# A fused attention, Fourier and MLP kernel: the last main row group is normalised behind its second product, under a new order of issue

## The chip, the cores and the metric

The kernel runs on one core of a Trainium2 chip. The metric is the device time of one launch in microseconds (us). The engines are TensorE (PE; its weight loads are shown as PEld), VectorE (DVE), ScalarE (ACT), GpSimd (POOL) and SyncE (SP), which only issues DMAs here.

## The reference, cut to what matters

```python
# q, k, v: (4, 4, 1088, 32); S1, S2: (8, 32); w_ch1: (128, 512); w_ch2: (512, 128)
phi  = lambda x: outer(S1 x, S2 x) per row, flattened to 64 features
kv   = einsum('bhsf,bhfd', phi(k), v);  z = sum over s of phi(k)
x    = (phi(q) kv) / (phi(q) z + 1e-6)        # laid out as (4, 1088, 128)
u    = x + real(fft(fft(x, axis=1), axis=2))
un   = (u - mean(u)) / sqrt(var(u) + 1e-6)    # over the 128 columns
out  = u + relu(un @ w_ch1) @ w_ch2           # (4, 1088, 128), float32
```

The mean is taken out by centring the first weight matrix (`cen`), so the kernel needs only the factor 1/sqrt(var + 1e-6) of each row, called its scale here. The scale is positive, so it may stand before or behind the ReLU.

## The kernel before, in words

There are four batches. For each batch b the kernel projects k (`kpr`), forms the 64 products of features (`kp`, four pieces), sums them against v on TensorE (`kv`, copied by `kvz`), does the same for q in two halves (`qf`, `qa`, `qp`), and multiplies both (`pnd`; `den`, `rden`, `x` divide). The Fourier step folds x over the columns and over the batch's two row halves (`df` and `eo`), multiplies with sine and cosine tables made on the chip (`s`), and copies the sum out (`z`); `zr` is its mirror for the second row half (two instructions of 272 columns), `zl` gathers the columns of the last rows (two small strided copies). The tables come from `t_turn`, `l_turn`, `d_turn` on POOL, `t_ph`, `l_ph`, `d_ph`, `t_pm`, `l_pm`, `d_pm` on DVE, and sines on ACT.

The MLP then works on ten groups g of rows. Groups 4 and 9 are the small last ones (128 rows each: the tails of two batches); the eight others are the main ones, 512 rows each; group 8 is the last main one (`TWO = 8`). For each group: `mix` adds x and the transform into PSUM (the tile is called u), `bn` and `var` take the statistics on DVE, `sd` a square root on ACT, `rc` a reciprocal on DVE, `un` writes u times the scale, rounded to bf16. The rounded rows are transposed: by a DMA for groups 0 to 6 (`xt`, line 635), by TensorE for 7, 8 and 9 (`tr`, then the copy `ut`). `ph` multiplies with the first weights, `rl` is the ReLU (each in two parts of 1024 columns), `po` multiplies with the second weights and adds onto u in PSUM, `fin` copies the sum to SBUF and `out` stores it. Group 8's u lies in two PSUM banks, so that its `po`, `fin` and `out` run in two halves.

PSUM has eight banks, and the table `BANK` says which bank a use has; a use waits until the bank's former readers are done. Nothing is scheduled at run time: the list `ORDER` is a written order of all steps, each engine gets its own steps in that order and runs them strictly so. `ENGINE` moves a step from its default engine. `FILL` puts multiplications of zeros ahead of a step on TensorE. `BEHIND` makes a load wait for an earlier load, `AFTER` makes one step wait for another without sharing data.

Of each engine's order before, what the change and the prediction touch: on PE `kv0 qf1.1 pnd0 kv1 qf2.1 pnd1 w1c qf3.1 kpr2 s0 ... po2 ph3.0 ph3.1 s3`; on DVE `bn0 var0 kvz2 rc0 un0 qp3.0`, with `zr0` on ACT and `zl0` on POOL; on POOL `kp3.1 kp3.0 kp3.3 kp3.2 w2b zl0`; at the end `mix8` on PE, then `bn8 var8 rc8 un8` on DVE with `sd8` on ACT, `tr8 ut8 ph8.1 rl8.1 ph8.0 ... po8.0 fin8.0 po8.1 fin8.1`.

Of the kernel before, what the change touches and what calls it, by code (L numbers as in the profile page):

```python
# [56 lines left out]
def program(nc, T, x, bank):  # L57
# [596 lines left out]
    def po(u, g, lo, hi):  # L654
        for t in range(lo, hi):
            for c in range(4):
                nc.tensor.matmul(ps(u, ut_at(g, t), [[1, 128]]), view(own("ht", g), (128 if g % 5 == 4 else 512) * c + 128 * t, [[1, 128]]),  # L657
                                 T("w2b")[:, c, :], start=False, stop=True, skip_group_check=True)
# [191 lines left out]
ld_vt1 c_kvz c_sgn kpr0.1 kt_pr c_v10 ld_q2.1 ld_v1.3 kt_ab kt_p qT1.0 ld_v1.0 qT1.1 ld_v1.1 ld_v1.2 ld_q2.0 qp0.1  # L850
ld_q3.1 kpr0.0 kab0 kp0.3 kp0.1 ld_k2 qt_T d_trig qf0.0 qa0.0 qp0.0 kT1 ld_q3.0 kp0.2 qf1.0 qa1.0 vc0 qt_f ld_w1 kp0.0
qp1.0 l_turn c_qtp kpr1 t_ph3 qt_a kab1 t_cos1 ld_v2.0 kv0 l_ph kvz0 kp1.1 vc1 qf1.1 ld_v2.3 qT2.1 ld_v2.1 ld_k3 qa1.1
qt_p kp1.2 t_sin1 kp1.3 ld_v2.2 l_pm l_sin pnd0 c_eo0 qT2.0 qT3.1 kp1.0 ld_v3.0 den0 kv1 c_eo2 c_eo1 kvz1 qp1.1 d_alt
qf2.1 rden0 x0 df0.1 kT2 qa2.1 l_cos pnd1 ld_v3.2 qT3.0 df0.0 den1 qp2.1 w1c eo0.0 ld_w2 w1b qf3.1 eo0.1 kpr2 qa3.1
kab2 rden1 x1 t_neg ld_v3.1 ld_v3.3 s0 qp3.1 kp2.0 qf2.0 kT3 vc2 kpr3 kp2.1 z0 kp2.3 mix0 kp2.2 qa2.0 df1.1 qp2.0
a_sqrt kv2 kab3 df1.0 eo1.0 bn0 eo1.1 zr0 kp3.1 kp3.0 qf3.0 var0 sd0 kvz2 rc0 un0 qa3.0 qp3.0 mix1 vc3 bn1 kp3.3 s1
var1 pnd2 sd1 z1 kp3.2 xt0 ph0.1 rl0.1 zr1 rc1 kv3 w2b zl0 den2 rden2 x2 df2.1 kvz3 df2.0 eo2.1 un1 ph0.0 mix2 xt1 zl1
rl0.0 bn2 var2 pnd3 eo2.0 sd2 rc2 s2 den3 rden3 x3 un2 z2 mix3 ph1.0 bn3 xt2 var3 po0 fin0 out0 rl1.0 sd3 ph1.1 ph2.0
rc3 un3 rl1.1 rl2.0 df3.0 zr2 df3.1 eo3.1 mix5 bn5 var5 zl2 ph2.1 rl2.1 po1 mix4 eo3.0 mix6 bn4 var4 sd5 po2 sd4 rc5
fin1 fin2 xt3 ph3.0 rl3.0 rc4 un4 un5 xt4 ph3.1 bn6 var6 sd6 rc6 xt5 un6 s3 z3 xt6 rl3.1 ph4.0 po3 zr3 rl4.0 ph5.0  # L860
rl5.0 po4 fin3 zl3 ph5.1 fin4 mix9 bn9 mix7 ph6.0 var9 rl5.1 sd9 bn7 out2 out3 out1 out4 rl6.0 var7 rc9 po5 un9 ph6.1
sd7 fin5 rc7 mix8 rl6.1 tr9 un7 ut9 ph9.0 tr7 rl9.0 po6 bn8 var8 ut7 sd8 rc8 fin6 ph7.0 rl7.0 un8 po9 out5 ph7.1 rl7.1
out6 fin9 tr8 ut8 ph8.1 rl8.1 ph8.0 out9 po7 fin7 out7 rl8.0 po8.0 fin8.0 po8.1 fin8.1 out8.1 out8.0
# [38 lines left out]
```

## Time and profile before

| What | us |
|---|---|
| median of the 3 runs (82.08, 82.40, 84.12) | 82.4 |
| the profiled execution, its own time | 82.32 |
| its span, from the first to the last instruction | 80.4 |
| busy: PE, PEld, DVE, ACT, POOL | 69.6, 52.0, 65.0, 49.5, 45.2 |

Of the 3 runs two lie within 0.4% of each other and one is 2.1% above the median. The profiled execution has 1.9 us around its span. PE is the busiest engine; a busy PE means that a matmul was in its pipeline, not that the array was full.

### The profile page before, as it was taken

What the parts mean: (1) busy time and instruction counts of PE and PEld (TensorE: products, weight loads), DVE (VectorE), ACT (ScalarE), POOL (GpSimd) and SP (SyncE); (2) the same over time, 40 slices, a digit from 0 to 9 for tenths busy, and PEclk for the clock granted to TensorE, in tenths of its full rate; (3) what the DMA queues carried; (4) which work ended last, traced back from release to release, by engine and by line L of the source; (5) the groups of instructions that cost most, each with busy time, mean ns of one, the idle gap of its engine ahead of it and who ended that gap; (6) DMA issues with size and microseconds to landing.
All of it is one profiled execution on the core that took longest, in us unless ns stands there. A gap on an engine that the chain in (4) does not pass through costs nothing.

```text
span 80.4 us, 3294 instructions
## 1 busy us (share of the span) xinstructions
PE 69.6 (87%) x1368; PEld 52.0 (65%) x1375; DVE 65.0 (81%) x178; ACT 49.5 (62%) x85; POOL 45.2 (56%) x84
## 2 busy tenths in 40 slices
...
GB/s 8 270 174 269 229 288 208 53 208 229 227 44 310 207 144 292 151 125 212 0 34 43 0 8 65 8 65 0 177 19 16 95 190 253 29 130 138 24 176 90
DMA packets 16095, 10.47 MB, mean 130 GB/s; under 512 B 6864, under 2 KB 14544, under 8 KB 16080
## 3 DMA queue, kind: packets, MB, share of 16 engines
...
q8 instruction: 10, 0.16, 0.8%
...
q14 instruction: 5, 0.04, 0.2%
HBM read 7.22 MB, written 2.23 MB: 117 GB/s over the span
## 4 chain that ended last, share of the span: by engine, by line
PE 48%; DVE 18%; DMA 11%; SPq 8%; ACT 7%; issue 4%; DVEq 0%; ACTq 0%
PE ps L481 9%; PE ps L395 8%; PE ps L435 7%; PE ps L657 6%; DMA t_qt_in<-in_q_dram 6%; PE ps L643 5%; DMA t_unT__166<-t_un__161 5%; PE ps L361 4%; SPq L141 3%; ACT t_ht__168 L650 3%; PE ps L521 2%; PE ps L458 2%; SPq L147 2%; DVE t_x__130 L496 2%; DVE t_x__131 L496 2%
## 5 line engine op out<-in xcount | busy, mean ns | idle before, releaser
L102 POOL TENSOR_TENSOR t_kp__119<-t_ab__117 128x512 f32<-128x512 f32 x7 | 7.3, 1068 | 1.5 <-ACT t_ab__117 L413 1.1
L650 ACT ACTIVATE t_ht__167<-ps 128x1024 bf16<-128x1024 f32 x6 | 6.0, 1022 | 1.6 <-PE ps L481 1.6
L102 POOL TENSOR_TENSOR t_kp__118<-t_ab__116 128x512 f32<-128x512 f32 x6 | 6.3, 1069 | 1.0 <-ACT t_ab__116 L413 1.0
L442 ACT COPY t_qa__122<-ps 128x1024 f32<-128x1024 f32 x4 | 4.1, 1013 | 3.1 <-DVE t_qp__124 L446 1.9
L650 ACT ACTIVATE t_ht__168<-ps 128x1024 bf16<-128x1024 f32 x4 | 4.1, 1024 | 2.9 <-PE ps L577 1.9
L442 ACT COPY t_qa__123<-ps 128x1024 f32<-128x1024 f32 x4 | 4.1, 1014 | 2.3 <-PE ps L435 2.3
L643 PEld LDWEIGHTS <-t_w1b 128*128 128x128 bf16 x40 | 3.0, 97 | 3.7 <-issue 1.5
L90 PE MATMUL ps<-t_wz 128*128 128x512 bf16 x12 | 5.0, 526 | 0.0
L481 PEld LDWEIGHTS ps<-t_kvz,t_qp__124 128*64 128x64 f32 x128 | 4.0, 137 | 0.9 <-ACT t_kvz L95 0.4
L481 PE MATMUL ps<-t_kvz,t_qp__124 128*64 128x66 f32 x128 | 4.4, 223 | 0.1
L395 PE MATMUL ps<-t_v__121,t_kp__119 128*64 128x33 f32 x128 | 4.3, 223 | 0.1
L102 POOL TENSOR_TENSOR t_eo__133<-t_xd__132 128x516 bf16<-128x516 bf16 x4 | 4.2, 1052 | 0.4 <-DVE t_xd__132 L102 0.3
L395 PEld LDWEIGHTS ps<-t_v__121,t_kp__119 128*64 128x64 f32 x128 | 4.1, 138 | 0.4 <-POOL t_zl__143 L96 0.4
L395 PE MATMUL ps<-t_v__120,t_kp__118 128*64 128x33 f32 x128 | 4.3, 223 | 0.0
L481 PEld LDWEIGHTS ps<-t_kvz,t_qp__125 128*64 128x64 f32 x128 | 3.9, 137 | 0.5 <-issue 0.4
L481 PE MATMUL ps<-t_kvz,t_qp__125 128*64 128x66 f32 x128 | 4.2, 223 | 0.0
L395 PEld LDWEIGHTS ps<-t_v__120,t_kp__118 128*64 128x64 f32 x128 | 4.1, 138 | 0.1
L650 ACT ACTIVATE t_ht__169<-ps 128x1024 bf16<-128x1024 f32 x4 | 4.0, 1027 | 0.0
L652 DVE TENSOR_SCALAR t_ht__168<-ps 128x1024 bf16<-128x1024 f32 x2 | 2.5, 1225 | 1.7 <-PE ps L657 1.0
L435 PE MATMUL ps<-t_qT__115,t_sa 32*64 32x256 f32 x64 | 2.8, 400 | 1.2 <-DVE t_qp__124 L446 1.2
L379 DVE STREAM_TRANSPOSE t_kT__112<-t_k_in__105 128x512 f32<-128x512 f32 (+1 forms) x3 | 2.7, 886 | 1.1 <-DMA t_k_in__105<-in_k_dram 1.1
L361 PE MATMUL ps<-t_sblk,t_kT__112 128*64 128x64 f32 x64 | 2.5, 226 | 1.1 <-DVE t_kT__112 L379 1.1
...
## 6 DMA issues: line engine op xcount, KB each, us to landing
...
```

Source lines behind the costliest of these rows:

```text
L90: nc.tensor.matmul(T("ps")[:, free, :], w[:, 0:128], bass.AP(tensor=w.tensor, offset=w.offset, ap=[list(w.ap[0]), [0, 4], [1, 128]]), star ...
L102: return (nc.vector if engine == DVE else nc.gpsimd).tensor_tensor(out=out, in0=in0, in1=in1, op=op)
L361: nc.tensor.matmul(ps(use, 64 * t, [[1, 64]], 64 * c, 64), view(src, 128 * t + 64 * c, [[1, 64]]), T("sblk")[:], start=True, stop=True, ti ...
L379: nc.vector.transpose(view(T(f"kT{b % 2}"), 128 * lo, [[1, 128 * n]]), view(T(f"k_in{b % 2}"), D * lo, [[D, n], [8 * D, 4], [1, D]]))
L395: nc.tensor.matmul(ps(f"kv{b}", 33 * pr, [[1, 33]], 64 * c, 64), kp, v, start=(t == 0), stop=(t == 8), tile_position=(0, 64 * c), skip_gro ...
L435: nc.tensor.matmul(ps(f"q{b}.{pr}", 512 * g + 256 * w, [[1, 256]], 64 * h, 64), view(T(src), 0, [[1, F]], 32 * g, 32), view(T(f"qT{b % 2}" ...
L442: nc.scalar.copy(T(f"qa{pr}")[:], ps(f"q{b}.{pr}", 0, [[512, 4], [1, 256]]))
L481: nc.tensor.matmul(ps(f"nd{b}", 512 * (s // 3) + 132 * (s % 3) + 66 * pr, [[1, 66]], 64 * c, 64), w, view(T("kvz"), 132 * b + 66 * pr, [[1 ...
L496: nc.vector.tensor_tensor(out=view(T(f"x{b}"), 0, [[384, 3], [32, 12], [1, 32]]), in0=ps(f"nd{b}", 0, [[512, 3], [33, 12], [1, 32]]), in1= ...
L643: nc.tensor.matmul(ps(use, 128 * n * i, [[1, 128 * n]]), T("w1b")[:, 128 * c:128 * c + 128], own("unT", g)[:, 0:128 * n], start=True, stop ...
L650: nc.scalar.activation(out=out, in_=in_, func=ACT.Relu)
L657: nc.tensor.matmul(ps(u, ut_at(g, t), [[1, 128]]), view(own("ht", g), (128 if g % 5 == 4 else 512) * c + 128 * t, [[1, 128]]), T("w2b")[:, ...
```

## The change

Group 8 is listed as late (`LATE = (8,)`). Its u lies in one bank. It is copied once in f32 to SBUF (`uc8`, into a buffer of k that is free by then) and once rounded to bf16 without the scale (`un8`, now one copy on ACT, which waits for `mix8` alone). The transpose, both products and the ReLU work on unscaled rows; the second product goes into two banks of its own (`p8.0`, `p8.1`), and `fin8.0`, `fin8.1` become two DVE instructions each, which multiply by the scale and add `uc8`. `FINE` is an option for the ReLU in quarters and is empty. `bn8`, `var8`, `sd8`, `rc8` stay, and are needed by `fin8` only.

Along with that the whole of `ENGINE`, `FILL`, `BEHIND`, `AFTER`, `ORDER` and `BANK` is replaced. Among the moves: `zr0` from ACT to DVE, `zl0` and `zl2` from POOL to DVE, `zl1` from DVE to POOL, `t_neg` from DVE to POOL, `z1` and `z2` from DVE to ACT, `un1 un4 un5 un8` to ACT, `vc2` to ACT and `vc3` to POOL, `c_eo1` to DVE, `fin2 fin5 fin6` to DVE, `fin7` to ACT, `w1c` behind `qf3.0`, `s3` ahead of `mix6` and of group 3's first product, and `mix8` ahead of `mix7`. The zero multiplications in bf16 become 18 (12 before); the one in f32 stays.

```diff
--- before.py
+++ after.py
@@ -26,10 +26,12 @@
 NB = NK // 2 + 1
 BY_DMA = (0, 1, 2, 3, 4, 5, 6)
 SPLIT = {}
-TURNS = {"un": 5, "unT": 5, "ht": 3, "ot": 4, "st": 5, "sm": 5}
+TURNS = {"un": 5, "unT": 5, "ht": 3, "ot": 4, "st": 5, "sm": 5, "uc": 1}
 NXD = 1
 WARM = 4
 TWO = 8
+LATE = (8,)
+FINE = ()
 MAGIC = float(1.5 * 2 ** 23)
 PI = float(np.pi)
 
@@ -562,15 +564,16 @@
 
     def ut_at(g, t):
 
-        return 128 * t if g != TWO else 512 * (t // 2) + 128 * (t % 2)
+        return 128 * t if g != TWO or g in LATE else 512 * (t // 2) + 128 * (t % 2)
 
     def u_all(g, n):
-        return [[128, n], [1, 128]] if g != TWO else [[512, 2], [128, 2], [1, 128]]
+        return [[128, n], [1, 128]] if g != TWO or g in LATE else [[512, 2], [128, 2], [1, 128]]
 
     def mix(b, half, g):
         u = f"u{b}.{half}"
-        for c in range(1 if g != TWO else 2):
-            w = 512 if g != TWO else 256
+        two = g == TWO and g not in LATE
+        for c in range(2 if two else 1):
+            w = 256 if two else 512
             nc.tensor.matmul(ps(u, 512 * c, [[1, w]]), T("idb")[:], view(T(f"x{b}"), 512 * half + w * c, [[1, w]]),
                              start=True, stop=False, skip_group_check=True)
         for t in range(4):
@@ -617,6 +620,9 @@
 
     def un(u, g, n, engine):
         sm, out = own("sm", g), own("un", g)
+        if g in LATE:
+            copy(engine, view(out, 0, [[1, 128 * n]]), ps(u, 0, [[1, 128 * n]]))
+            return
         if engine == DVE:
             two = [[256, 2], [128, 2], [1, 128]] if g == TWO else [[128, n], [1, 128]]
             by = [[2, 2], [1, 2], [0, 128]] if g == TWO else [[1, n], [0, 128]]
@@ -651,13 +657,21 @@
         else:
             nc.vector.tensor_relu(out, in_)
 
-    def po(u, g, lo, hi):
-        for t in range(lo, hi):
-            for c in range(4):
-                nc.tensor.matmul(ps(u, ut_at(g, t), [[1, 128]]), view(own("ht", g), (128 if g % 5 == 4 else 512) * c + 128 * t, [[1, 128]]),
-                                 T("w2b")[:, c, :], start=False, stop=True, skip_group_check=True)
+    def po(u, g, tiles, chunks=range(4), at=0):
+
+        for t in tiles:
+            for c in chunks:
+                where = ut_at(g, t) if g not in LATE else 128 * (t - at)
+                nc.tensor.matmul(ps(u, where, [[1, 128]]), view(own("ht", g), (128 if g % 5 == 4 else 512) * c + 128 * t, [[1, 128]]),
+                                 T("w2b")[:, c, :], start=g in LATE and c == 0, stop=c == 3, skip_group_check=True)
 
     def fin(u, g, lo, hi, engine):
+        if g in LATE:
+            for t in range(lo, hi):
+                nc.vector.scalar_tensor_tensor(
+                    out=own("ot", g)[:, 128 * t:128 * t + 128], in0=ps(u, 128 * (t - lo), [[1, 128]]), scalar=own("sm", g)[:, t:t + 1],
+                    in1=own("uc", g)[:, 128 * t:128 * t + 128], op0=ALU.mult, op1=ALU.add)
+            return
         copy(engine, own("ot", g)[:, 128 * lo:128 * hi], ps(u, ut_at(g, lo), [[1, 128 * (hi - lo)]]))
 
     def st_half(b, half, g, c):
@@ -675,8 +689,9 @@
     def mixer(b, half, g, reads):
         u, n = f"u{b}.{half}", (4 if half < 2 else 1)
         o = f"l:{g // 5}" if n == 1 else f":{g - g // 5}"
-        use_u = u + (":2" if g == TWO else "")
-        pairs = ((0, 1), (2, 3)) if n == 4 else ((0, 1, 2, 3),)
+        late = g in LATE
+        use_u = u + (":2" if g == TWO and not late else "")
+        pairs = ((0, 1, 2, 3),) if n == 1 else ((0,), (1,), (2,), (3,)) if g in FINE else ((0, 1), (2, 3))
         nb = len(pairs[0]) if n == 4 else 1
         whole = (f"ht{o}/0 ht{o}/1") if n == 1 else ""
         e = lambda what, default: eng(f"{what}{g}", default)
@@ -685,7 +700,9 @@
         add(f"var{g}", e("var", DVE), f"st{o}", f"va{o}", lambda: var(g, n, e("var", DVE)))
         add(f"sd{g}", ACTE, f"va{o} eps tabsqrt", f"sd{o}", lambda: sd(g, n))
         add(f"rc{g}", DVE, f"sd{o} va{o}", f"rc{o}", lambda: rc(g, n))
-        add(f"un{g}", e("un", DVE), f"rc{o} pu:{g}", f"un{o}", lambda: un(u, g, n, e("un", DVE)), use_u)
+        if late:
+            add(f"uc{g}", e("uc", ACTE), f"pu:{g}", f"uc{o}", lambda: copy(e("uc", ACTE), own("uc", g)[:, 0:128 * n], ps(u, 0, [[1, 128 * n]])), use_u)
+        add(f"un{g}", e("un", DVE), f"pu:{g}" if late else f"rc{o} pu:{g}", f"un{o}", lambda: un(u, g, n, e("un", DVE)), use_u)
         if g in BY_DMA:
             add(f"xt{g}", SP, f"un{o}", f"unT{o}", lambda: xt(g, n))
         else:
@@ -697,15 +714,29 @@
             add(f"ph{g}.{i}", PE, f"unT{o} w1b", f"ph_:{g}/{i}", lambda i=i, cs=cs: hid(f"h{g}.{i}", g, n, cs), use)
             add(f"rl{g}.{i}", r, f"ph_:{g}/{i}", whole or f"ht{o}/{i}",
                 lambda i=i, cs=cs, r=r: relu(f"h{g}.{i}", g, n, cs, r), use)
+        ready = " ".join(f"ht{o}/{i}" for i in range(len(pairs) if n == 4 else 2)) + f" w2b un{o}"
+        scale = f" uc{o} rc{o}" if late else ""
         if g == TWO:
             for c in range(2):
-                add(f"po{g}.{c}", PE, f"ht{o}/0 ht{o}/1 w2b un{o}", f"pu2:{g}/{c}", lambda c=c: po(u, g, 2 * c, 2 * c + 2), use_u)
-                add(f"fin{g}.{c}", eng(f"fin{g}.{c}", DVE), f"pu2:{g}/{c}", f"ot{o}/{c}",
-                    lambda c=c: fin(u, g, 2 * c, 2 * c + 2, eng(f"fin{g}.{c}", DVE)), use_u)
+                p = f"p{g}.{c}" if late else use_u
+                if g not in FINE:
+                    add(f"po{g}.{c}", PE, ready, f"pu2:{g}/{c}", lambda c=c, p=p: po(p if late else u, g, range(2 * c, 2 * c + 2), at=2 * c), p)
...
+            for c in range(2):
+                p = f"p{g}.{c}" if late else use_u
+                done = " ".join(f"pu2:{g}/{i}" for i in range(4)) if g in FINE else f"pu2:{g}/{c}"
+                add(f"fin{g}.{c}", eng(f"fin{g}.{c}", DVE), done + scale, f"ot{o}/{c}",
+                    lambda c=c, p=p: fin(p if late else u, g, 2 * c, 2 * c + 2, eng(f"fin{g}.{c}", DVE)), p)
                 add(f"out{g}.{c}", (SP, ACTE)[c], f"ot{o}/{c}", f"out/{g}/{c}", lambda c=c: st_half(b, half, g, c))
             return
-        add(f"po{g}", PE, f"ht{o}/0 ht{o}/1 w2b un{o}", f"pu2:{g}", lambda: po(u, g, 0, n), u)
-        add(f"fin{g}", e("fin", DVE), f"pu2:{g}", f"ot{o}/0 ot{o}/1", lambda: fin(u, g, 0, n, e("fin", DVE)), u)
+        p = f"p{g}" if late else u
+        add(f"po{g}", PE, ready, f"pu2:{g}", lambda: po(p, g, range(n)), p)
+        add(f"fin{g}", e("fin", DVE), f"pu2:{g}" + scale, f"ot{o}/0 ot{o}/1", lambda: fin(p, g, 0, n, e("fin", DVE)), p)
         add(f"out{g}", SP, f"ot{o}/0 ot{o}/1", f"out/{g}",
             (lambda: st_main(b, half, g)) if n == 4 else (lambda: st_last(b, g)))
 
@@ -803,6 +834,8 @@
     made["eo2"] = made["ph"][:].bitcast(BF16)
     for i in range(2):
         made[f"htl{i}"] = made["lpm"][:, 256 * i:256 * i + 256].bitcast(BF16)
+
+    made["uc0"] = made["k_in0"][:, 0:512]
     x = {"q": q, "k": k, "v": v, "S1": S1, "S2": S2, "w1": moe_w_ch1, "w2": moe_w_ch2, "out": out}
     steps = {s.name: s for s in program(nc, made.__getitem__, x, BANK.__getitem__)}
     order = ORDER.split()
@@ -825,48 +858,49 @@
 
 
 ENGINE = {
-    "c_vt0": "DVE", "c_v11": "DVE", "c_vt1": "DVE", "vc0": "ACT", "vc1": "ACT", "kp1.3": "DVE", "den0": "ACT", "den1":
-    "ACT", "kp2.1": "DVE", "kp2.3": "DVE", "df1.1": "DVE", "zr0": "ACT", "kvz2": "DVE", "vc3": "ACT", "z1": "DVE",
-    "zr1": "ACT", "df2.1": "DVE", "zl1": "DVE", "eo2.0": "DVE", "un2": "ACT", "z2": "DVE", "df3.1": "DVE", "fin1":
-    "ACT", "fin2": "ACT", "z3": "DVE", "zr3": "DVE", "rl5.0": "DVE", "fin3": "ACT", "fin4": "ACT", "fin5": "ACT",
-    "ut9": "DVE", "ut7": "DVE", "fin6": "ACT", "ut8": "DVE", "rl8.1": "DVE", "fin8.0": "ACT", "fin8.1": "ACT",
+    "c_eo1": "DVE", "c_xd0": "DVE", "c_vt0": "DVE", "c_vt1": "DVE", "c_sgn": "DVE", "vc0": "ACT", "kp1.0": "DVE",
+    "vc1": "ACT", "den0": "ACT", "t_neg": "POOL", "den1": "ACT", "vc2": "ACT", "kp2.1": "DVE", "d_alt": "DVE", "zr0":
+    "DVE", "zl0": "DVE", "zr1": "ACT", "df2.1": "DVE", "df2.0": "DVE", "un1": "ACT", "eo2.0": "DVE", "un2": "ACT",
+    "df3.0": "DVE", "fin1": "ACT", "un4": "ACT", "z3": "DVE", "un5": "ACT", "zl2": "DVE", "fin4": "ACT", "un8": "ACT",
+    "uc8": "DVE", "fin3": "ACT", "var7": "POOL", "ut9": "DVE", "ut8": "DVE", "rl6.1": "DVE", "rl7.0": "DVE", "fin7":
+    "ACT",
 }
 FILL = {
-    "warm": (1, 1, 6), "qf0.1": (0, 2, 6), "qf0.0": (0, 3, 6), "kpr1": (0, 1, 7), "po8.0": (0, 1, 0),
+    "s_t": (1, 2, 0), "qf0.0": (0, 3, 0), "qf0.1": (0, 3, 0), "qf1.0": (0, 2, 4), "kt_pr": (0, 1, 3), "kv1": (0, 1,
+    7), "qf3.1": (0, 1, 4), "ph3.1": (0, 1, 7),
 }
 BEHIND = {
-    "ld_q1.1": 6, "ld_v0.1": 6, "ld_v1.1": 6, "ld_v1.2": 5, "ld_q2.0": 6, "ld_k2": 2, "ld_w1": 3, "ld_v2.0": 3,
-    "ld_v2.3": 4, "ld_k3": 6, "ld_v2.2": 4, "ld_v3.0": 4, "ld_v3.2": 2, "ld_w2": 4,
+    "ld_v0.0": 5, "ld_v0.1": 6, "ld_vt0": 6, "ld_q2.1": 6, "ld_v1.3": 3, "ld_q2.0": 6, "ld_q3.1": 5, "ld_v2.2": 4,
+    "ld_v2.1": 6, "ld_v2.0": 5, "ld_w1": 2, "ld_w2": 4, "ld_v3.1": 4, "ld_v3.2": 5,
 }
 AFTER = {
-    "t_turn0": "t_ph2", "d_turn": "t_pm0", "kt_p": "d_pm", "kp1.1": "l_ph", "kp1.0": "l_pm", "df1.0": "df1.1",
-    "df2.0": "df2.1", "eo3.1": "df3.1",
+    "d_turn": "t_ph1", "kp0.3": "t_ph2", "kp1.1": "d_pm", "eo2.1": "eo2.0", "df3.1": "df3.0",
 }
 
 ORDER = """
...
+c_wz warm ld_q0.0 c_iota c_rows ld_q0.1 ld_s1 c_bias c_eo1 a_sin ld_s2 c_xd0 ld_k0.1 c_vt0 c_more c_vt1 c_kk t_turn1
+t_turn3 c_idb t_ph3 ld_k0.0 ld_q1.0 ld_q1.1 ld_v0.0 qT0.0 c_id16 s_t t_ph1 c_cen c_mask qT0.1 s_use ld_qt c_v10 kT0.1
+ld_v0.3 ld_kt kT0.0 qf0.0 ld_k1 ld_v0.2 kpr0.1 ld_v0.1 ld_vt0 c_v11 ld_vt1 d_turn qa0.0 t_turn2 l_turn ld_v1.0 qT1.0
+kpr0.0 ld_q2.1 t_ph2 kab0 qp0.0 qT1.1 qf0.1 c_kvz t_cos1 t_sin1 c_sgn kp0.3 ld_v1.3 kp0.1 qa0.1 ld_v1.2 qf1.0 qa1.0
+qt_T ld_v1.1 ld_q2.0 qp0.1 kt_T kp0.0 qp1.0 kT1 ld_q3.1 kt_pr ld_q3.0 ld_k2 kt_ab qt_f qt_a vc0 ld_v2.3 kp0.2 ld_v2.2
+ld_v2.1 t_turn0 ld_k3 qf1.1 kt_p qa1.1 d_ph l_ph kpr1 kab1 ld_v2.0 c_qtp t_ph0 t_pm0 l_pm d_pm t_cos0 kv0 c_eo0 qt_p
+qT2.1 kp1.0 kvz0 qp1.1 l_cos pnd0 t_sin0 vc1 kp1.1 ld_w1 ld_w2 qT2.0 ld_v3.1 ld_v3.3 ld_v3.2 kp1.2 kp1.3 den0 rden0 x0
+qT3.0 ld_v3.0 qT3.1 kv1 l_sin d_trig c_eo2 t_neg kT2 qf2.1 df0.0 kvz1 qa2.1 pnd1 a_sqrt den1 kpr2 qp2.1 qf3.1 rden1 x1
+kab2 df0.1 eo0.1 eo0.0 kp2.2 qa3.1 kT3 vc2 kp2.3 kp2.0 qp3.1 s0 df1.1 df1.0 eo1.1 kpr3 z0 qf2.0 eo1.0 kp2.1 kab3 qa2.0
+d_alt mix0 qp2.0 bn0 vc3 var0 kv2 zr0 qf3.0 kp3.3 kvz2 sd0 kp3.0 rc0 zl0 w1c kp3.2 un0 qa3.0 s1 qp3.0 w1b mix1 pnd2
+xt0 z1 zr1 ph0.1 kp3.1 w2b bn1 var1 sd1 rc1 kv3 den2 rden2 zl1 x2 df2.1 df2.0 un1 mix2 eo2.0 rl0.1 ph0.0 kvz3 bn2 var2
+pnd3 rl0.0 xt1 sd2 rc2 den3 eo2.1 s2 rden3 x3 un2 df3.0 ph1.0 df3.1 eo3.0 eo3.1 z2 xt2 mix3 bn3 var3 ph1.1 rl1.0 po0
+fin0 ph2.0 rl1.1 sd3 mix4 rc3 bn4 po1 var4 rl2.0 sd4 zr2 mix5 ph2.1 fin1 un3 xt3 rc4 un4 xt4 rl2.1 s3 bn5 var5 sd5 rc5
+z3 mix6 un5 zl2 out1 bn6 var6 ph3.1 xt5 rl3.1 po2 fin2 sd6 rc6 ph4.0 rl4.0 zr3 zl3 un6 ph3.0 mix8 bn8 po4 rl3.0 out2
+mix7 bn7 fin4 ph5.0 mix9 un8 bn9 var9 po3 uc8 rl5.0 sd9 rc9 xt6 fin3 out0 un9 var8 ph5.1 rl5.1 var7 tr9 out3 sd7 tr8
+ut9 ph9.0 rl9.0 ph6.0 out4 po5 rl6.0 ut8 rc7 ph8.0 po9 ph6.1 un7 fin5 out5 rl8.0 tr7 ph8.1 fin9 out9 ut7 ph7.0 rl6.1
+rl7.0 rl8.1 ph7.1 po6 po8.0 rl7.1 po7 fin6 sd8 out6 rc8 fin8.0 out8.0 po8.1 fin8.1 fin7 out8.1 out7
 """
 BANK = dict(x.split("=") for x in """
-wm=0 st=1 w1=7 kt=5 k0=4 kv0=7 k1=4 kv1=4 k2=7 kv2=7 k3=4 kv3=4 qt=5 q0.0=4 q0.1=0 nd0=5 z0=5 u0.0=5 h0.0=6 h0.1=6
-u0.1=0 h1.0=3 h1.1=6 q1.0=0 q1.1=0 nd1=4 z1=6 u1.0=1 h2.0=3 h2.1=6 u1.1=2 h3.0=6 h3.1=0 u0.2=3 h4.0=0 q2.0=0 q2.1=0
-nd2=1 z2=6 u2.0=5 h5.0=6 h5.1=0 u2.1=4 h6.0=6 h6.1=0 q3.0=1 q3.1=0 nd3=2 z3=6 u3.0=3 t7=0 h7.0=0 h7.1=4 u3.1=6 t8=2
-h8.0=4 h8.1=1 u1.2=2 t9=5 h9.0=5
+wm=1 st=1 w1=2 kt=0 k0=1 kv0=0 k1=7 kv1=3 k2=0 kv2=0 k3=3 kv3=7 qt=1 q0.0=4 q0.1=0 nd0=0 z0=1 u0.0=3 h0.0=0 h0.1=0
+u0.1=2 h1.0=6 h1.1=0 q1.0=4 q1.1=3 nd1=1 z1=0 u1.0=4 h2.0=6 h2.1=6 u1.1=5 h3.0=2 h3.1=2 u0.2=0 h4.0=7 q2.0=4 q2.1=4
+nd2=4 z2=0 u2.0=1 h5.0=2 h5.1=2 u2.1=6 h6.0=2 h6.1=2 q3.0=4 q3.1=4 nd3=5 z3=2 u3.0=7 t7=1 h7.0=0 h7.1=2 u3.1=4 t8=5
+h8.0=4 h8.1=4 p8.0=5 p8.1=6 u1.2=0 t9=4 h9.0=4
 """.split())
```

23 lines of the change are left out of this document (6 added, 17 removed).

## The prediction

> **What bounds the kernel now.** First the page's busy times and its chain of work that ended last, by engine:
>
> ```profile
> PE 69.6 (87%) x1368; PEld 52.0 (65%) x1375; DVE 65.0 (81%) x178; ACT 49.5 (62%) x85; POOL 45.2 (56%) x84
> ...
> PE 48%; DVE 18%; DMA 11%; SPq 8%; ACT 7%; issue 4%; DVEq 0%; ACTq 0%
> ```
>
> No single engine sets the time, so it has to be read by stage. The busy times in stretches (sum, then PE, PEld, DVE, ACT, POOL):
>
> ```profile
> 17.00:33.00 16.00, 15.94 (x463) 13.39 (x464) 14.51 (x20) 9.96 (x19) 10.87 (x21) 1.00 0.77 219
> 33.00:43.00 10.00, 9.79 (x237) 7.95 (x236) 8.78 (x22) 7.05 (x11) 9.10 (x10) 1.00 0.40 87
> 43.00:53.00 10.00, 9.62 (x252) 8.62 (x250) 9.08 (x29) 5.16 (x12) 5.05 (x8) 1.00 0.08 17
> 53.00:65.00 12.00, 10.50 (x129) 7.90 (x130) 9.88 (x41) 8.69 (x14) 6.10 (x10) 1.00 0.29 70
> 65.00:80.40 15.40, 10.76 (x117) 7.50 (x119) 8.89 (x31) 9.46 (x16) 0.20 (x1) 1.00 0.36 129
> ```
>
> From 17 to 53 us PE has no gap: there whatever delays one PE step moves everything behind it. Behind 53 us PE waits, and DVE and ACT hand work round; there a shorter chain can pay. The chain in order of time, near its end, says for what:
>
> ```profile
> 61.13 4.07 DMA t_unT__166<-t_un__161
> ...
> 73.37 0.44 DVE t_unT__164 L96
> ...
> 76.06 1.08 PE ps L657 x16
> 77.14 0.02 issue
> 77.17 0.37 ACT t_ot__173 L95
> ```
>
> Last I read the timeline for instructions that took longer than others of their kind. This decides my forecast:
>
> ```profile
> 5.14 0.45 DVE L224 TENSOR_SCALAR t_pm<-t_ph 128x548 int32<-128x548 int32 x1
> ...
> 20.60 1.18 DVE L224 TENSOR_SCALAR t_lpm<-t_lph 128x546 int32<-128x546 int32 x1
> ...
> 20.97 0.52 POOL L99 MEMSET t_eo__133<- 128x504 bf16 x1
> ...
> 48.11 1.27 POOL L102 TENSOR_TENSOR t_xd__132<-t_x__130 128x567 bf16<-128x567 bf16 x1
> 48.19 1.23 DVE L96 COPY t_zl__144<-t_z__136 128x32 bf16<-128x32 bf16 x1
> ...
> 49.33 0.17 DVE L96 COPY t_zl__144<-t_zr__140 128x32 bf16<-128x32 bf16 x1
> ...
> 64.24 0.69 DVE L545 TENSOR_SCALAR t_zr__142<-t_z__138,t_sgn 128x272 bf16<-128x272 bf16 x2
> 64.27 0.21 POOL L96 COPY t_zl__146<-t_z__138 128x32 bf16<-128x32 bf16 x1 [4.77 <-DVE t_z__138 L96]
> ```
>
> `l_pm` takes 1.18 us where `t_pm0`, of the same size, took 0.45, and ends 0.29 behind POOL's memset (21.49). The copy of 32 columns takes 1.23 instead of 0.17 and ends 0.04 behind POOL's 1.27 us instruction. So some DVE instructions that read and write only SBUF wait until a running POOL instruction is through.
>
> **The change, part by part.** The sum is made against the profiled execution, 82.32 us with a span of 80.4; that is 0.1% below the median of 82.4.
>
> *The start: +0.6.* DVE has `s_use` behind `t_ph3`, which waits for two POOL turns instead of one (0.51 + 0.43 each, from 1.86: 3.9), then 0.50, 0.71 (`qT0.0`), 0.50 (`t_ph1`), 0.71: `s_use` at 6.4, the first `qf` at 6.85 (6.50 before). SP issues `k`'s first halves ahead of `kt` (128 KB), so `kT0` may run to 9.2 and `qT1.0` start at 9.4, when its load, one load earlier in the queue, should be there (10.38 before). From 9.4 DVE is one chain up to `kT1`: 0.71, 0.50, 1.18, 0.71, 0.10, 0.68, 1.20, 0.45, 1.20, 1.23, by the rows of L428, L221, L446, L452, L371 and L379: 17.4. `kpr1` (1.15) and `kv0` (2.25) follow, then `kvz0` (0.45) and hand-overs: `pnd0` at 21.9, 21.27 before, with the same PE work done ahead of it, `qf1.1` included. Bounds: +1.6 if that load lands as late as before; -1.0 since POOL's pieces of `kp0` would end at 14.75 instead of 15.77 and DVE's chain might be shorter. I take +0.6, the chain by rows.
>
> *Zero multiplications: +0.4.* Two of them (`kv1`, `qf3.1`) now stand in the stretch without gaps; three in a row took 0.82 less 0.39 for the last's drain, so 0.215 each. Those in the start fall into PE's waits, and the one at `ph3.1` stands where PE waits for a transposing DMA; uncovered, 0.2 each.
>
> *`w1c` (1.05): 0.* It moves behind `qf3.0`, on the same engine; `w1b` (0.59 on ACT) is wanted first by `ph0.1`, a `pnd` (2.5) later.
>
> *`zr0`, `zl0` on DVE: +2.3.* By the durations of before, `bn0` and `var0` end at about 40.4. POOL then starts `vc3` (1.06), `kp3.3 kp3.0 kp3.2 kp3.1` (1.03 apart) and `w2b` (0.61) without a gap, 40.1 to 46. `zr0` and `zl0` are four instructions in SBUF (0.39, 0.39, 0.2, 0.2 undisturbed). Queued behind them on DVE are `un0` (0.69) and `qp3.0` (1.2), and `pnd2`, with all PE work behind it, needs `qp3.0`. Undisturbed that ends at 43.1, ahead of PE (44.3): 0. If only the `zl0` copies wait, each for the running POOL instruction: about 45.3, +1.0. If all four do, one getting in at each boundary: 41.5, 42.85, 43.95, 45.05, then `un0` 45.75 and `qp3.0` 46.95: +2.7. If none gets in before POOL's queue is empty (`l_pm` did not get in at the boundary at 21.0): 46.2 + 1.2 + 0.69 + 1.2, +4.9. Nothing excludes a small gain for POOL, at most 0.2. The rows leave open whether `zr` is of the waiting sort: 0.37 to 0.42 us beside a POOL copy that took its usual 0.21 speaks against it. I take all four, 2.7, less 0.4 that later waits absorb (for group 3's DMA).
>
> [...]
>
> *`s3` ahead of group 2's and 3's products: -1.2.* Between the ends of `s2` (52.8) and `s3` (63.38) before, PE had 8.8 us of work, counting 0.22 for a product of 512 columns and 0.056 for one of 128: 1.8 idle. After, `s3` needs only `fin1` and `eo3`, both early; I count 7.1 us for 6.6 of work, 0.5 idle. Bounds: 0 and -1.8.
>
> *`zl2` on DVE: +0.3.* It starts with POOL's `zr3` (1.05 each) when `z3` ends; one copy may wait 0.8, and `bn6`, `fin2`, `mix8` behind it. Between 0 and 0.8.
>
> *Group 8: -0.1.* Before, from `bn8` (70.05) to the end of `un8` (72.47) it took 2.4 us; now one ACT copy of 512 columns (0.59). PE's idle on that way was 0.5 (`ut8`) and 0.4 (last ReLU), so -0.9 at most. Against it: `uc8` on DVE (0.69, as `fin` from PSUM), ahead of `rc9` and `un9`; and `fin8`. A multiply-and-add of 128 columns from PSUM has no row: between 0.22 (`bn`, one in a row of four) and 0.31 (L221, 128 columns in SBUF), so 0.5 for the last two against 0.37 on ACT: +0.15. ACT's `fin7` (0.59) and store order add up to 0.4, because SP's `out7` is now last and ACT's `out8.1` stands behind `fin7`. With all groups' ReLUs nearer together ACT has 15.6 us of work in the last 19. Net between -0.9 and +0.6.
>
> Sum: 0.6 + 0.4 + 2.3 - 1.2 + 0.3 - 0.1 = 2.3, so 84.6 us. A measurement of this kernel can tell about 2% (80.75 to 84.05) from no change.
>
> **The rivals.**
>
> *DVE is not held up.* Without the 2.3: 82.3, no change. For it: `zr`'s row, and that a POOL instruction may have to wait instead. Against it: three slow DVE instructions of that kind, the third being `t_neg` (0.89 at 31.69, ending 0.29 behind POOL).
>
> *Faster: PE's waits behind `s2` go.* From 52.8 to the last product at 77.13 PE had 24.3 us for 19.5 of work (counted as above), 4.8 idle; I count 3.5 idle for the changed kernel, since ACT and DVE hand each group on. Group 8 needs neither now ahead of its transpose but one copy, and the smaller groups stand between the larger ones. If only 1.0 of idle is left, and DVE isn't held up, it is 82.3 - 2.5 = 79.8; it counts as faster from 1.9 of idle on. For it: the chain before runs through `ut8` and the last ReLU (73.37, 76.06). Against it: the ten ReLU parts of 1.02 to 1.23 us behind `s3` stay, and ACT and DVE are as full there as before.
>
> *DVE starves.* `zr0` waits for POOL's last `kp3`: +4.9 instead of 2.3, 87.2. For it: `l_pm`. It needs that POOL never yields between two instructions.
>
> *PE's clock drops at the start.* The zero products stood 0.43 us apart at 2.9 to 4.2 us and 0.215 at 10.3, at a granted clock of 1.00 throughout, so PE is slow at first. My longest PE wait is 13.0 to 14.95. If it slowed PE again for as long as at first (some 3.4 us), half of that is lost: 1.7, so 86.3 with the rest. No row shows a second slow spell. [...]
>
> **How the numbers follow.** Forecast 0.42; not held up 0.24; faster 0.16; starving 0.13; slow clock 0.05. The forecast's own range, with the start's and tail's bounds, is 83.0 to 86.4. Only its lowest part, 0.05 or so, is within 2%, and a tenth of the rival "not held up" lies above. Faster 0.16, within 2% 0.27, slower 0.57. The range over the cases runs from 80.8, which leaves out most of the faster case, to 87.3.
>
> **What would show it.** In the changed profile: `zr0` or `zl0` on DVE (L547, L98) over 0.6 us beside POOL's L104 and `vc3`; PE idle ahead of `pnd2` (L483) behind `qp3.0`; `pnd0` at about 21.9; `s3` (L523, its fourth round) ending with less than 1 us of PE idle since `s2`; fin8's four instructions at 0.22 to 0.31. Wrong would be: `zr0` and `zl0` at 0.4 and 0.2 with no PE gap there, a start off by over 1 us, or a last stage (from the end of `s3`) that is over 1 us from 15.9.

## The result: slower by 9%, three times the loss that was forecast

The changed kernel takes 89.64 us (four runs, 88.95 to 89.95) against 82.24 for before (four runs): a ratio of 1.0907, 95% interval 1.0804 to 1.1009. Forecast were 84.6 us, with 80.8 to 87.3 as the range. The profiled execution took 89.34 with a span of 87.3. Its mean granted clock is 0.961 (1.000 before). The medians here and below are over all executions of a kernel; the ratios leave out those more than about 1.5% above its fastest, among them executions of before of 85.6 to 87.2 us with a mean granted clock of 0.92 to 0.96.

First the page of after: busy times, PE and its granted clock in 40 slices of 2.18 us, and the chain by engine.

```profile
PE 73.7 (84%) x1380; PEld 53.4 (61%) x1380; DVE 63.8 (73%) x185; ACT 52.2 (60%) x94; POOL 49.6 (57%) x78
...
PE   5950399978997999989999779999999998898920
...
PEclk9999555899999999999999999999999999999999
...
PE 46%; ACT 16%; DVE 14%; DMA 14%; issue 3%; POOL 1%; SPq 1%; DVEq 0%; ACTq 0%
```

PE is busy 4.1 us longer than before although it was given only six more short zero products: its clock stands at half from 8.94 to 15.76 (the mean granted clock is 0.85 from 8.90 to 8.95, and 0.69 from 15.70 to 15.80). Ahead of that is a hole, the `0` in PE's row. By stretches of after (sum, then PE, PEld, DVE, ACT, POOL, granted clock, DMA share, GB/s):

```profile
0.00:17.00 17.00, 11.40 (x103) 5.32 (x111) 9.53 (x36) 4.42 (x8) 8.46 (x29) 0.80 0.78 186
17.00:33.00 16.00, 14.40 (x403) 11.44 (x387) 13.32 (x22) 11.28 (x22) 13.86 (x16) 1.00 0.66 192
...
43.00:53.00 10.00, 8.94 (x214) 7.13 (x213) 8.41 (x25) 5.46 (x13) 8.78 (x11) 1.00 0.08 16
53.00:65.00 12.00, 11.66 (x236) 9.38 (x233) 9.81 (x34) 8.35 (x18) 3.78 (x4) 1.00 0.25 25
65.00:87.30 22.30, 17.53 (x206) 12.34 (x203) 15.54 (x56) 15.62 (x29) 5.86 (x12) 1.00 0.44 121
```

The hole's cause stands at the head of the chain that ended last (start us, us, what):

```profile
1.78 2.85 DMA t_s<-in_S_dram
4.63 0.02 issue
4.65 5.26 DMA t_s<-in_S_dram
9.91 0.14 issue
10.04 0.25 PE ps L341
...
45.91 2.11 DVE t_zr__139 L547 x2
...
48.08 0.96 DVE t_zl__143 L98 x2
49.04 0.59 DVE t_un__157 L629
49.64 1.14 DVE t_qp__125 L448
...
50.82 2.33 PE ps L483 x72
```

The load of S1 (SP) lands at 4.63, and only then does ACT issue the load of S2, at 4.65; it lands at 9.91. Before, S2 was issued at 1.62, ahead of S1 (start, us, engine, line):

```profile
1.62 0.58 ACTq L106 DMA_DIRECT2D t_s<-in_S_dram  x1
1.78 0.45 SPq L106 DMA_DIRECT2D t_s<-in_S_dram  x1
...
5.19 0.28 PE L339 MATMUL ps<-t_id,t_s 16*128 16x16 f32 x1
```

Everything on PE behind the first zero products needs both: `s_t` makes the matrix that all feature products use. The built program, not the trace, says why ACT waits: in after, S2's DMA instruction waits for the third of the eight semaphores on which DMAs report their landing, the one that S1's load uses; before, it waits for none. The later pieces are the step that the forecast gave 2.3 us: `zr0` and `zl0` on DVE (3.2 us in all), then `un0`, `qp3.0`, and `pnd2` on PE. PE's waits in after, longest first (us in total, times, longest):

```profile
PE ps L341 <- DMA t_s<-in_S_dram: 4.6, 1, 4.6
PE ps L483 <- DVE t_qp__125 L448: 1.1, 1, 1.1
```

Landmarks in the profiled executions, each in the clock of its own run; "s2 first" is the experiment x1 below, which is after without that wait:

| | before | forecast | after | s2 first |
|---|---|---|---|---|
| `s_use` starts | 6.13 | 6.4 | 10.41 | 6.03 |
| `pnd0` starts | 21.27 | 21.9 | 26.88 | 20.36 |
| `pnd0` to `pnd2` | 21.45 | 24.15 | 23.94 | 23.05 |
| `pnd2` to the last product's end | 34.41 | 33.4 | 32.78 | 32.90 |
| from there to the end of the time | 5.19 | 5.2 | 5.74 | 6.67 |
| sum | 82.32 | 84.6 | 89.34 | 82.98 |

The miss is 4.7 us in the profiled executions. The row of `pnd0` alone has 5.0; the other rows together come to 0.3 less than forecast.

### The profile page after: what moved, and what is told of

Same layout as the page of the kernel before. It is cut to its first block, busy times and chain, and to the rows that moved or that the text cites. A ratio compares the mean times of both kernels' runs of the same rounds, so it can differ in the third digit from the quotient of the medians.

```text
span 87.3 us, 3321 instructions
## 1 busy us (share of the span) xinstructions
PE 73.7 (84%) x1380; PEld 53.4 (61%) x1380; DVE 63.8 (73%) x185; ACT 52.2 (60%) x94; POOL 49.6 (57%) x78
## 4 chain that ended last, share of the span: by engine, by line
PE 46%; ACT 16%; DVE 14%; DMA 14%; issue 3%; POOL 1%; SPq 1%; DVEq 0%; ACTq 0%
DMA t_s<-in_S_dram 9%; PE ps L483 8%; PE ps L437 7%; PE ps L649 6%; PE ps L665 6%; PE ps L397 5%; DMA t_unT__166<-t_un__161 4%; PE ps L363 4%; ACT t_ht__168 L656 4%; PE ps L92 3%; DVE t_qp__124 L448 3%; DVE t_zr__139 L547 2%; ACT t_qa__123 L444 2%; PE ps L523 2%; PE ps L460 2%
## 5 line engine op out<-in xcount | busy, mean ns | idle before, releaser
L104 POOL TENSOR_TENSOR t_kp__118<-t_ab__116 128x512 f32<-128x512 f32 x7 | 7.3, 1068 | 7.7 <-ACT t_ab__116 L415 7.7
L92 PE MATMUL ps<-t_wz 128*128 128x512 bf16 x18 | 7.5, 512 | 1.9 <-DVE t_wz L173 1.0
L104 POOL TENSOR_TENSOR t_kp__119<-t_ab__117 128x512 f32<-128x512 f32 x7 | 7.4, 1085 | 1.9 <-ACT t_ab__117 L415 1.9
L656 ACT ACTIVATE t_ht__168<-ps 128x1024 bf16<-128x1024 f32 x6 | 6.0, 1022 | 0.7 <-PE ps L649 0.7
L656 ACT ACTIVATE t_ht__167<-ps 128x1024 bf16<-128x1024 f32 x5 | 5.1, 1022 | 1.5 <-DVE t_st__147 L596 0.8
L448 DVE TENSOR_TENSOR t_qp__124<-ps,t_qa__122 128x1024 f32<-128x1024 f32 x2 | 2.4, 1224 | 3.3 <-ACT t_qa__122 L444 3.3
L92 PEld LDWEIGHTS <-t_wz 128*128 128x128 bf16 x18 | 1.7, 115 | 4.4 <-issue 3.1
L448 DVE TENSOR_TENSOR t_qp__124<-ps,t_qa__123 128x1024 f32<-128x1024 f32 x2 | 2.4, 1224 | 2.4 <-ACT t_qa__123 L444 2.4
L97 ACT COPY t_kvz<-ps 64x66 f32<-64x66 f32 x8 | 1.7, 209 | 3.9 <-PE ps L397 3.4
```

The source lines that it names most:

```text
L92: nc.tensor.matmul(T("ps")[:, free, :], w[:, 0:128], bass.AP(tensor=w.tensor, offset=w.offset, ap=[list(w.ap[0]), [0, 4], [1, 128]]), star ...
L104: return (nc.vector if engine == DVE else nc.gpsimd).tensor_tensor(out=out, in0=in0, in1=in1, op=op)
L448: nc.vector.tensor_tensor(out=view(T(f"qp{b % 2}"), 1024 * pr, [[32, 4], [128, 8], [1, 32]]), in0=ps(f"q{b}.{pr}", 256, [[512, 4], [32, 8] ...
L656: nc.scalar.activation(out=out, in_=in_, func=ACT.Relu)
```

## The experiments

Two theories at the outset. T1: the late load of S2, with the half clock that follows, is the 5 us. T2: the start is absorbed later, since DVE, POOL and the loads bind there anyway, and the loss lies in `zr0`, `zl0`, `t_neg` and the new order.

**x1: S2's load ahead of the table step.**

```diff
-c_wz warm ld_q0.0 c_iota c_rows ld_q0.1 ld_s1 c_bias c_eo1 a_sin ld_s2 c_xd0
+c_wz warm ld_q0.0 c_iota c_rows ld_q0.1 ld_s1 c_bias c_eo1 ld_s2 a_sin c_xd0
```

> After, with the load of S2 put on ACT's queue ahead of the sine-table step instead of behind it; in this order its issue no longer waits for the landing of S1, everything else as in after. Theory T1 (the late load: S2 is issued at 4.65 instead of 1.62, lands at 9.91, the PE stands 5.4 us, and the half clock that follows makes the start longer still; together +5.0 of the +7.3): s_t starts at 5.0 to 5.6, no slice at half clock, pnd0 at 21.5 to 22.5 instead of 26.88, total 84.0 to 85.2, that is the forecast of 84.6. Rival T2 (the folding's waits bind anyway and absorb the start; the loss lies in zr0 and zl0 on DVE, t_neg on POOL, a_sqrt ahead of den1 and the new order): S2 lands early, pnd0 early too, but the end stays at 87.5 to 89.5.

82.94 us (82.80 to 82.98), ratio to before 1.0096 (1.0036 to 1.0155); clock 1.0, `s_t` at 5.42, `pnd0` at 20.36. T2 is out: nothing of the lateness is regained later. The gain of 6.4 between the profiled executions is even more than T1 asked for. (PE's stand in after is the 4.6 us of the list above, not 5.4: that is how long its weight loads paused.) `pnd0` is here 0.9 us earlier than before; but x7 below, whose start is that of before, has it at 20.24, so this landmark moves by 1 us from one execution to the next.

**x2: the same wait put into before.** S2's load gets a dependency on S1's; the rest is before.

```diff
+            if name == "ld_s1":
+                wait(sent["ld_s2"][0], sent["ld_s1"][0])
```

> Before, with one wait added: the load of S2 on ACT's queue waits for the landing of S1, as it does in after; nothing else changed. T1: S2 issued at 4 to 5, landing near 9 to 10, s_t near 9 to 10, two or three slices at half clock, pnd0 at 25 to 27 instead of 21.27, total 86.3 to 88.0. T2: s_t late too, but the lateness is taken up later in the kernel: 82.3 to 84.5.

86.93 us (86.75 to 87.85), ratio 1.0608 (1.0467 to 1.0749). The page of that run, PE and its clock:

```profile
PE   5920799929999999999999999999997979797910
...
PEclk9998556999579999999999999999999999999999
```

S2 is issued at 4.61, `s_t` runs at 9.23, `pnd0` at 26.61. The clock is at half from 7.79 to 14.61, and in this execution, the longest of the four, once more from 21.4 to about 24.8, behind a stand of PE of 1.6 us at 17.4. One wait, and nothing else of the change, costs before 6% by the ratio, some 5 us; on before's side only two executions, 81.86 and 82.39 us, stand in that ratio. Taken away from after or put into before, it makes the difference.

**x9: the wait gone, the order of each queue kept.** In x1 S2 also went out earlier than all loads. Here the three constants, the table step and S2's load are only written earlier in the list; the queues issue as in after, but for three small memsets on DVE, and the load of `v0.0` waits for one earlier load more.

```diff
-c_wz warm ld_q0.0 c_iota c_rows ld_q0.1 ld_s1 c_bias c_eo1 a_sin ld_s2 c_xd0
+c_wz warm c_bias a_sin ld_s2 ld_q0.0 c_iota c_rows ld_q0.1 ld_s1 c_eo1 c_xd0
```

> After with two steps written earlier in the order (the three constants on DVE and with them the table step and S2's load on ACT). Each queue issues what it issued in after, S2 still behind the table step on ACT and all of SP's loads in the same order; only the three small memsets stand one place earlier on DVE. What changes is the semaphore on which S2 reports its landing: in after it is the one that S1's load uses, so S2 waits for S1; here it is one of its own. If that wait alone is the cause: S2 issued at 1.6 to 2.2 instead of 4.65, s_t at 5.0 to 5.7, clock 1.0, total 82.5 to 83.5, as with S2 put ahead of the table step. Rival (S2 gained there by going out first of all loads, ahead of the bulk of SP's queue, not by losing the wait): landing still at 7 to 10, s_t at 7 or later, total 85 to 89.

83.19 us (82.83 to 83.41), ratio 1.0122 (1.0012 to 1.0232). The timeline of that run (start, us, engine, line):

```profile
1.04 0.58 ACTq L108 DMA_DIRECT2D t_s<-in_S_dram  x1
1.77 0.45 SPq L108 DMA_DIRECT2D t_s<-in_S_dram  x1
...
5.39 0.23 PE L341 MATMUL ps<-t_id,t_s 16*128 16x16 f32 x1
```

S2 goes out at 1.04, earlier than I had expected (1.6 to 2.2), and so still ahead of most of SP's loads. The wait alone is the cause of the late issue: x2 has it with nothing else changed, and x9 is without it. It isn't a matter of data: both loads write to parts of one tile in before, x9 and after alike. It comes with the semaphore that the load is given when the program is built, and that changed with the place of the load in the written list (in x9 S2 reports on the fourth, S1 on the third). How much of the 5.26 us that S2 took to land in after (2.85 for S1) is due to the bulk loads ahead of it wasn't tried by itself.

**x4 and x5: the lateness without the half clock.** 22 instead of 2 zero products ahead of `s_t` keep PE at work while it waits for S2 (in x5 it is busy for all 5.00 us from 5 to 10); x5 also has 5 instead of 2 ahead of `qf1.0`.

```diff
-    "s_t": (1, 2, 0), ... "qf1.0": (0, 2, 4),
+    "s_t": (1, 22, 0), ... "qf1.0": (0, 5, 4),
```

> After as it is, S2 late, but with 22 instead of 2 short zero-matmuls ahead of s_t on PE, so that PE works through most of the stretch from 5.4 to 9.9 in which it stood; they compute nothing that is used. Clock part of T1 (the stand itself drops the granted clock to 0.5 for some 8 us): no slice at half clock, s_use still near 10.4, pnd0 0.8 to 2.0 earlier than 26.88, total 87.6 to 88.9. Rival (the half clock costs nothing, since the start waits on loads and DVE; lateness alone is the whole +5): pnd0 at 26.6 to 27.0, total 89.3 to 89.9.

> The kernel of 22 zero-matmuls ahead of s_t, with S2 as late as in after, and now 5 instead of 2 zero-matmuls ahead of qf1.0 as well, so that PE stands under 0.5 us instead of 0.84 before the step kt_pr, behind which x4_clock_kept had its clock at half from 19.8 to 22.5. Nothing else. If the half clock is the larger part of what after lost: granted clock 1.0 throughout, s_use near 10.4, pnd0 at 24.0 to 24.8 (26.88 in after), total 85.0 to 86.2, as in the one of the four times of x4_clock_kept that was at 85.25. If the lateness alone is the larger part: pnd0 at 25.5 or later and total 87.0 to 88.5.

x4 took 85.25 to 87.63 us; its profiled execution, 86.97, has `s_use` at 10.35 and `pnd0` at 25.91, and a half clock of its own, from 19.8 to 22.5 at the least, behind a stand of PE of 0.84 us at 16.5. x5 took 86.38 to 89.83 (median 87.27); its profiled execution, at 86.75, kept the clock:

```profile
PE   5999899999979999899999499998999699898920
...
PEclk9999999999999999999999999999999999999998
```

With `s_use` at 10.62, later still than in after, `pnd0` starts at 24.82 instead of 26.88. So of the 6.4 us between after (89.34) and x1 (82.98) the half clock has 2.6 (89.34 - 86.75) and the lateness 3.8, by this one execution; `pnd0`'s 2.1 is of the same size. The other executions with a clock of 0.999 or 1.0, x4's 85.25 and x5's 86.38 and 87.78, would give the half clock 4.1, 3.0 and 1.6. That the half clock costs nothing is out; which of the two parts is the larger these executions don't tell.

**x3 and x6: `zr0` and `zl0` back.** x1 with `zr0` on ACT and `zl0` on POOL behind `w2b`; x6 has x5's five zero products ahead of `qf1.0` as well.

```diff
-    "zr0": "DVE", "zl0": "DVE",
+    "zr0": "ACT",
-rc0 zl0 w1c ... w2b bn1 var1
+rc0 w1c ... w2b zl0 bn1 var1
```

> The first of these four kernels (S2 ahead of the table step) with zr0 back on ACT and zl0 back on POOL, behind w2b, as before had them. The forecast's largest term (two zr0 and the first zl0 on DVE beside POOL's run hold un0 and so qp3.0 and pnd2 up by 2.7, less 0.4): 1.9 to 2.7 less than that kernel, 81.6 to 82.8; pnd2 at most 21.5 after pnd0 instead of 23.9. Rival (what DVE loses there PE would wait for anyway, for instance behind w1b's and kp3's POOL run): within 0.6 of that kernel.

> S2 ahead of the table step, zr0 on ACT and zl0 on POOL as in x3_s2_first_zr0_act, and 5 instead of 2 zero-matmuls ahead of qf1.0, which shorten PE's stand of 1.0 us before kt_pr to some 0.4. If a stand of 1 us is what took the clock to half 2.5 us later (15.75 to 18.95 in that kernel's profile): clock 1.0, pnd0 at 20.2 to 20.6 instead of 21.80, total 80.8 to 81.5, faster than before by over 1%. Rival (the clock drops for another reason, or the three matmuls push qp1.0 and with it the chain): pnd0 near 21.5, 82.0 to 83.0.

x3: 80.97 to 83.37 us, ratio to before 0.9876 (0.9719 to 1.0033). x6: median 82.55, ratio 0.9979 (0.9914 to 1.0044). Neither is shown to beat before. Against x1 (82.94) x3's median of 81.88 is 1.1 less, and its two lowest times (80.97 and 81.25) are 1.7 to 2.0 less; 1.9 to 2.7 were expected. x6's profiled execution kept its clock and had `pnd0` at 20.51, as expected, but the total of 80.8 to 81.5 did not come. What `zr0` and `zl0` cost is read in the timelines. x1, with both on DVE:

```profile
38.48 2.13 DVE L547 TENSOR_SCALAR t_zr__139<-t_z__135,t_sgn 128x272 bf16<-128x272 bf16 x2
39.30 4.28 POOL L104 TENSOR_TENSOR t_kp__119<-t_ab__117 128x512 f32<-128x512 f32 x4
40.59 0.95 DVE L98 COPY t_zl__143<-t_z__135 128x32 bf16<-128x32 bf16 x1
41.46 0.17 DVE L98 COPY t_zl__143<-t_zr__139 128x32 bf16<-128x32 bf16 x1
...
42.15 1.21 DVE L448 TENSOR_TENSOR t_qp__125<-ps,t_qa__122 128x1024 f32<-128x1024 f32 x1
...
43.41 0.40 PE L483 MATMUL ps<-t_kvz,t_qp__124 128*64 128x66 f32 x6 [1.00 <-DVE t_qp__125 L448]
```

And x6, with both back:

```profile
41.19 1.23 DVE L448 TENSOR_TENSOR t_qp__125<-ps,t_qa__122 128x1024 f32<-128x1024 f32 x1 [0.31 <-ACT t_qa__122 L444]
...
43.40 0.40 PE L483 MATMUL ps<-t_kvz,t_qp__124 128*64 128x66 f32 x6
```

`qp3.0` starts 0.23 behind the start of `s1` instead of 2.24, and PE's wait of 1.00 ahead of `pnd2` is gone: from the start of `s1` to `pnd2` it is 2.44 us instead of 3.50. The hold-up is real and worth 1.0 to 1.1, less than the 1.9 to 2.7 expected. Up to `pnd2` x6 still gains nothing by it (43.40 and 43.41), since its `s0` began 5.66 behind `pnd1` (4.96 in x1): a load of k for `kT2` let DVE wait 1.22 there (0.55 in x1). x3's profiled execution shows the clock once more, behind a short stand of PE:

```profile
12.24:13.25 1.01, 0.01 (x2) 0.03 (x1) 1.01 (x2) 0.90 (x1) 1.01 (x2) 1.00 0.81 237
13.25:15.75 2.50, 2.50 (x58) 2.09 (x65) 2.50 (x4) 0.46 (x3) 2.33 (x5) 0.95 0.58 120
15.75:18.95 3.20, 3.20 (x58) 2.44 (x46) 3.17 (x10) 2.47 (x3) 0.91 (x2) 0.51 0.76 201
```

PE stood for 1.0 us, worked for 2.3, and then ran at half clock for 3.4 (from 15.50, hence the 0.95 in the second row, to 18.91). In x6, with that stand at 0.4, the clock stayed.

**x8: `zr0` and the first `zl0` on DVE in before.**

```diff
-    "zr0": "ACT", ... w2b zl0 den2 ...
+    "zr0": "DVE", "zl0": "DVE", ... w2b den2 ... rc0 zl0 un0
```

> Before with zr0 and the first half of zl0 moved to DVE, where the change has them, and nothing else. Forecast's largest term (two zr0 of 1.1 beside POOL's run instead of 0.35, the first zl0 of 0.9 to 1.0, all ahead of un0 and qp3.0 on DVE): pnd2 21.4 after pnd0 before, now 22.4 to 24.1 after it, total 83.3 to 85.0. Rival (the hold-up needs the new order too: here POOL's run does not stand beside them, or PE waits there anyway): pnd2 at most 21.9 after pnd0, total 82.0 to 82.8.

Median 84.26 us, ratio 1.0021 (0.9956 to 1.0087): no difference that this measurement tells. The profiled execution has the step, though: two `zr0` in 2.22 us, `pnd2` 23.05 behind `pnd0` (21.45 before), of which 0.94 lies between `s0` and `s1` (about half a wait for DVE's `kT3`, ahead of `zr0`; the rest where PE needs the second `zr0`) and 0.58 behind `s1`, where PE waits for `qp3.0`; its clock was at half from 15.85 to 19.26, ahead of `pnd0` at 22.15. Here the first `zl0` took 0.20 beside POOL's `kp3` run (4.22 from 42.05); in x1 it took 0.95 beside that run. The times leave the size open.

**x7: the late scale alone.** Before's tables, with `LATE = (8,)`, `un8` on ACT behind `mix8`, `uc8` on DVE behind `ut8`, `fin8` on DVE, and banks 7 and 6 for its second product.

```diff
+LATE = (8,)
-sd7 fin5 rc7 mix8 rl6.1 ... rl7.0 un8 po9 ... tr8 ut8 ph8.1
+sd7 fin5 rc7 mix8 un8 rl6.1 ... rl7.0 po9 ... tr8 ut8 uc8 ph8.1
```

> Before's tables and order, with the one edit that gives the change its name: group 8 is rounded and transposed unscaled (un8 on ACT behind mix8, uc8 on DVE behind ut8), its scale and the sum come in behind the second product (fin8 on DVE, two banks of their own). Forecast's term for it, -0.9 to +0.6: 81.3 to 82.9, last product at 76.3 to 77.5 (77.13 before). Rival (the copy of 512 columns that is added, 0.66, and ACT's rounding, 0.58, hold up relus that PE waits for): last product at 77.9 or later, 83.0 to 83.8.

Median 83.3 us, ratio 1.0115 (1.0037 to 1.0193): the edit that names the change costs some 0.9 us by itself (0.3 to 1.6 by the interval). That is far from the forecast's -0.1, and above its bounds of -0.9 to +0.6 but for the low end of the interval. The last product ended at 77.16, not at the 77.9 or later that the rival asked for, but `pnd0` had begun 1.0 earlier than before; so the stretches at the end have to be compared. The timeline of x7 says where:

```profile
68.98 0.58 ACT L97 CAST t_un__159<-ps 128x512 bf16<-128x512 f32 x1
...
69.47 1.03 ACT L656 ACTIVATE t_ht__169<-ps 128x1024 bf16<-128x1024 f32 x1
...
70.55 0.38 PE L637 MATMUL ps<-t_idb,t_un__158 128*128 128x128 bf16 x4 [0.56 <-ACT t_ht__169 L656]
...
76.75 0.87 DVE L671 SCALAR_TENSOR_TENSOR t_ot__173<-ps,t_sm__154,t_k_in__105 128x128 f32<-128x128 f32 x3 [0.15 <-PE ps L665]
...
77.95 0.38 ACTq L678 DMA_DIRECT2D out_dram<-t_ot__173  x1
```

The early rounding (0.58) stands on ACT ahead of a ReLU, and PE, which needs that ReLU's bank, waits 0.56. From the end of `s3` to the last product it is 14.24 us, 13.75 before. And the last store is issued at 77.95, 0.79 behind the last product's end, against 0.44 before (77.57 and 77.13): two multiply-and-adds of 0.3 take the place of one copy of 0.37. In this order `tr8` stays behind `ph7.1`, so the early rounding has nothing to give. After's order does use it (`tr8` ahead of `tr7`), but no run has that order without the late scale.

## Why the prediction was right in direction and wrong in size

- **The start, +0.6: wrong, +5.6.** This is the failed step. It took `s_use` from DVE's chain (6.4) and took for granted that both S loads land as before: the sum has no term for them. What S2's load waits for on its queue wasn't read from the changed program, although nothing but this one wait had to be found. The runs showed S2 issued at 4.65 instead of 1.62, `s_use` at 10.41 and `pnd0` at 26.88. Without it (x1) `s_use` starts at 6.03 and `pnd0` at 20.36, -0.9, at the low end of the bounds of -1.0 to +1.6; how much of that is chance is open, since it moves by 1 us.
- **"PE's clock drops at the start", 0.05 and 1.7 us: it happened, and cost some 2 to 4.** The case was made small because the longest wait in my own sum was 2 us; before kept a clock of 1.00 behind its stand of 1.2 (12.22 to 13.45), and that it would do so behind one of 2 us was my estimate. The 3.4 us of the term are PE's slow spell at first in before, seven zero products in bf16 from 2.92 to 6.43 (3.4 us busy, 0.40 to 0.43 us apart, at a granted clock of 1.00); that a later spell would be as long was an estimate too. With S2 late PE stood from 5.48 to 10.04, and the clock fell at 8.94, 3.5 us into the stand. The half clock lasted 6.82 us, until 15.76, with PE at work throughout from 10.04 on (5.72 of 5.72 us). x3 lost the clock behind a stand of only 1.0 us, for 3.4 (15.50 to 18.91).
- **`zr0`, `zl0` on DVE, +2.3: the hold-up came, the size was too large.** PE waits 1.0 to 1.1 us ahead of `pnd2` (after and x1), and x6 removes it. That all four instructions wait was my choice among the cases, and each was priced at one POOL instruction; three were long (1.06, 1.06 and 0.95 in x1, against the forecast's 0.39, 0.39 and 0.2 without a wait), the last took 0.17. In x1 the three ran beside POOL's copy of v (1.05 from 38.29) and its `kp3` run (4.28 from 39.30); but x8 has a `zl0` of 0.20 beside `kp3`, and no run takes POOL's run away, so that POOL holds them up isn't shown. The stretch from `pnd0` to `pnd2` came out at 23.94, forecast 24.15, partly by chance: 23.05 in x1.
- **Zero products, +0.4, and `w1c`, 0:** not tested alone; x1's stretch from `pnd0` to `pnd2` is 1.6 longer than before, 1.0 of it the wait above, which leaves 0.6 for them and the rest.
- **`s3` earlier, -1.2, `zl2`, +0.3, group 8, -0.1: together -1.0, measured -1.6** (34.41 to 32.78 and, in x1, 32.90). Between the ends of `s2` and `s3` PE's idle time fell from 1.3 to 0.3 us by the trace; the forecast had counted 1.8 and 0.5. `zl2` wasn't held up (0.16 and 0.17): it got in ahead of POOL's `zr3`, which started 0.1 behind the end of `z3`. The stage from the end of `s3` to the last product took 15.5, forecast 15.9. Group 8's term by itself was too low: +0.9 in x7. If it costs as much in the new order, which no run shows, the moves around it gained more than was forecast for them; which of them wasn't tested.
- **Not foreseen and of little effect:** `t_neg` on POOL takes 3.00 us (28.89), where DVE took 0.89 before; the next step on POOL starts at 31.83, and its input was complete at 31.50, so it was at most 0.3 late.
- "DVE starves", the rival that stood at 87.2 and so nearest to the result, is out: `pnd2` waited 1.1, not 4.9. Its number was near by accident.
